# A new order of work, five residual buffers and one output tile in two halves, in a retention-then-gMLP kernel on one core

## The chip, the cores and the metric

The kernel runs on one core of one Trainium2 chip. The metric is the device time of one execution in microseconds (us); a smaller time is better. The time of the kernel before is the median of 11 runs.

## The reference

Two layers, one after the other. The first is a retention layer: for 8 batches and 8 heads, with sequences of 576 rows and head dimension 64, scores of q and k are weighted with a decaying causal mask and multiplied with v. Its result, with the heads put side by side, is x, of 576 rows by 512 columns for each batch. The second is a gMLP block on x.

```python
scores = scale * np.matmul(q, k.transpose(0, 1, 3, 2))
Dmat = np.where(rel >= 0, gamma[:, None, None] ** rel[None, :, :], 0.0)
attn = np.matmul(scores * Dmat[None], v)
x = attn.transpose(0, 2, 1, 3).reshape(B, S, H * D)
h = gelu_tanh(x @ w_in)                      # 512 -> 1024
u, vv = h[..., :512], h[..., 512:]
v_n = layer_norm(vv) * g_ln
v_s = np.einsum('ts,bsd->btd', w_sg, v_n) + b_sg[None, :, None]
out = x + (u * v_s) @ w_out                  # 512 -> 512
```

All inputs and the output are float32; the kernel computes the products in bfloat16 and adds up in float32.

## The kernel before, in words

**Tiling.** The 8 batches are taken in 4 pairs p = 0 to 3. A pair has 1152 rows, that is 9 row tiles of 128, so there are 36 row tiles i = 0 to 35 in all (tile i belongs to pair i // 9). The retention layer works in 5 blocks for each pair, b = 0 to 19 in all. Four blocks of a pair cover 256 rows of one batch; the third one (b = 2, 7, 12, 17) covers the last 64 rows of one batch and the first 64 of the other.

**The steps.** The texts below name them so:
- load: the rows of q, k or v of one block go from DRAM to a tile `ld` (lines 431 and 434; 12 buffers). prep: GpSimd (POOL) scales and casts them to bfloat16 (lines 457 and 463; VectorE and ScalarE do q and k of block 0).
- T(b), copied by Tev: TensorE transposes q and k (line 503), VectorE copies the result from PSUM to `qkT` (line 512). From block 15 on (TB = 15), a DMA transpose TX(b) on SP's queue does both (line 519).
- S(b,g): scores (line 543); VectorE multiplies them with the mask, Sev (lines 556 and 559). Z(b): the running state of keys times values (line 577), with its sums on VectorE. O(b) and O2(b): the output of the block (line 626). Oev: ScalarE copies it to `xT` (line 682), which holds the x of a whole pair, transposed, in 2 buffers.
- V(i) and U(i): the two halves of x @ w_in (lines 693 and 740); ScalarE applies gelu (lines 700 and 750). VectorE takes the statistics (708), POOL turns them into scale and bias (713 to 716), ScalarE normalizes (728, and 725 for the tile in which the two batches of a pair meet).
- W(e,c,half): the product with w_sg (line 759); VectorE multiplies it with u, Wg (line 769).
- out(i): the product with w_out (line 786). For pair 0, x is added by TensorE (line 781). For tiles 9 to 35, X(i), a DMA transpose on SP's queue (line 795), brings the x of the tile back to row order, into `xr`, and VectorE adds it while it copies from PSUM, Oev of the output (line 802). `xr` has three buffers. store(i): SP's queue writes the finished tile of 128x512 float32 to DRAM (line 806).
- The five pieces of w_sg are loaded (lines 388 and 393), cast by ScalarE (line 397), transposed on TensorE (line 867, "builds of wT") and copied by VectorE (871). w_in comes in two halves: the half for V (in `wst`) and the half for U (in `uT`), each cast half by VectorE (371) and half by ScalarE (373).

**What sets the order.** Every step is a job with an engine, its dependencies and the buffers that it takes. A planner in the kernel's source (class `Planner`) can order them by a cost model. Here it doesn't: a string `ORDER` of 900 numbers is given, and each engine executes its jobs in the sequence in which their numbers stand in the string. Each engine, and SP's queue too, takes its instructions strictly in that sequence, so that a job that waits holds up all jobs behind it on its engine. Items like "f13" in the string are fillers: matmuls on a constant tile (line 338) that keep TensorE busy while nothing else can be done. PSUM gives the steps T, S and O two double-bank buffers ("pp") and all other TensorE steps four single-bank ones ("d").

Of the kernel before, what the change touches and what calls it, by code (L numbers as in the profile page):

```python
# [15 lines left out]
Alu = mybir.AluOpType  # L16
# [3 lines left out]
FETCH = ((32000.0, 7200.0), (130000.0, 6000.0), (1e9, 4800.0))  # L20
# [5 lines left out]
    '0 f9 1 2 81 8 111 83 6 f11 84 112 7 82 114 113 85 115 3 f2 87 13 86 116 122 118 117 278 f13 17 119 120 12 88 279 '  # L26
    'f3 280 121 281 9 123 282 23 124 f5 283 24 284 4 298 5 127 299 14 128 300 285 22 129 89 288 130 125 126 132 133 '
    '11 301 25 10 134 302 286 291 303 287 136 289 32 80 304 33 135 293 137 290 313 294 292 295 f2 15 90 f1 16 139 34 '
    '131 314 305 140 36 138 311 306 296 307 321 143 318 35 322 144 319 145 312 308 324 320 323 360 309 141 146 361 '
    '297 328 310 362 325 329 142 315 148 326 37 19 f4 149 18 21 363 327 20 38 152 364 330 366 91 99 92 95 365 97 100 '  # L30
    '26 93 316 98 373 147 43 96 317 94 370 153 374 367 331 154 27 39 150 380 151 42 371 375 155 368 381 332 376 156 '
    '334 333 369 342 40 382 335 343 157 372 383 338 384 158 377 340 385 28 41 430 339 341 161 29 159 163 431 389 44 '
    '379 160 336 390 386 378 162 164 46 107 387 392 47 337 31 388 347 432 391 30 433 393 348 45 166 396 108 434 167 '
    '351 435 172 436 49 349 397 344 165 350 352 398 50 354 345 173 101 174 355 170 102 168 353 171 450 48 440 179 451 '
    '437 441 504 169 452 443 438 180 439 453 444 51 175 442 58 454 105 456 394 106 455 447 176 470 182 53 177 188 449 '
    '465 178 471 472 395 457 183 466 356 189 463 458 346 448 508 459 460 190 464 357 461 181 473 358 186 474 359 187 '
    '109 476 445 475 52 54 110 103 446 477 56 104 462 184 478 191 185 467 516 399 59 517 414 400 197 518 416 192 468 '
    '409 57 469 407 415 410 198 60 519 417 195 536 520 537 206 401 521 408 405 196 522 523 402 427 479 524 406 482 '
    '193 428 200 194 429 480 62 199 201 403 481 529 404 525 526 207 530 418 527 528 538 419 483 202 420 591 203 539 '
    '63 215 421 55 540 592 61 533 411 422 541 542 217 593 534 424 216 66 412 545 543 535 544 209 67 546 204 210 425 '  # L40
    '484 550 208 68 205 548 551 547 594 549 71 485 213 552 631 595 214 488 596 492 632 423 489 597 500 633 64 493 553 '
    '611 501 211 222 218 212 413 598 531 612 599 231 76 554 600 502 496 613 490 503 532 486 219 223 491 601 426 487 '
    '65 224 614 602 225 603 615 604 617 226 78 608 616 75 621 605 606 232 609 622 220 227 221 607 618 70 228 494 619 '
    '634 495 677 73 620 229 240 635 626 678 505 230 627 233 637 509 679 506 636 561 623 497 242 510 573 511 498 69 '
    '562 680 507 241 234 575 697 628 681 698 624 683 512 574 682 559 243 258 610 565 560 625 690 248 566 629 235 557 '
    '630 638 249 684 639 691 640 236 685 238 499 692 558 643 567 239 687 251 237 641 688 555 686 642 693 699 556 246 '
    '752 247 700 576 701 702 753 513 644 77 689 568 577 694 709 569 579 514 254 710 244 570 256 695 703 245 72 250 '
    '706 704 255 578 696 571 587 707 711 705 754 515 645 572 583 712 708 563 74 661 713 79 647 662 564 755 646 257 '
    '715 648 252 772 253 259 756 588 757 773 580 758 714 759 581 262 589 584 657 760 774 765 665 585 263 651 766 582 '
    '762 264 590 652 761 265 726 763 663 727 764 732 649 769 775 650 664 260 792 733 776 724 777 794 270 658 793 725 '  # L50
    '744 770 666 659 778 586 271 779 771 667 261 273 655 780 716 656 734 717 795 735 268 781 838 796 745 797 839 798 '
    '799 269 787 668 800 746 660 782 801 748 653 783 747 804 767 788 673 784 785 654 669 789 805 266 274 749 275 840 '
    '272 768 674 267 786 670 790 675 791 802 750 671 740 276 803 858 277 841 736 720 859 722 676 728 860 723 721 842 '
    '751 861 843 718 672 844 845 719 862 853 848 854 846 806 849 847 741 863 729 850 737 807 855 742 864 730 818 738 '
    '814 856 731 822 743 865 808 834 857 823 815 812 809 826 810 867 811 739 813 824 866 868 816 825 819 817 869 870 '
    '820 874 827 871 821 835 830 828 876 872 836 875 837 851 873 829 883 889 852 879 897 881 880 884 877 882 831 878 '
    '890 832 833 898 891 901 887 899 892 895 888 900 893 896 909 885 894 905 886 902 910 903 904 906 911 907 912 908 '
# [8 lines left out]
class Job:  # L66
    def __init__(self, eng, dur, due, fn, deps=(), new=None, uses=(), mode=None, nbytes=0, run=0, what="", behind=None, since=0.0, lag=0.0, ins=0, port=False, parts=1):
        self.what, self.behind, self.since, self.lag, self.ins, self.port, self.parts = what, behind, since, lag, ins, port, parts
        self.eng, self.dur, self.due, self.fn = eng, dur, due, fn
        self.deps = [d for d in deps if d is not None]  # L70
        self.new = [] if new is None else list(new) if isinstance(new, (list, tuple)) else [new]
        self.mode, self.nbytes, self.run = mode, nbytes, run
        self.start = self.out = None
        for b in uses:
            b.users.append(self)
        for b in self.new:
            b.users.append(self)


class Planner:  # L80


    def __init__(self, bufs, free, slack=60.0, penalty=500.0, fill=None, fill_until=0.0):
        self.bufs, self.free = bufs, free
        self.slack, self.penalty = slack, penalty
        self.fill, self.fill_until = fill, fill_until
        self.jobs, self.order = [], {t: [] for t in bufs}
        self.dma_free, self.dmas, self.ring = 0.0, [], []
        self.mode, self.warm = None, False
        self.count, self.block, self.landed = 36, 1, 0.0  # L90
        self.port = 0.0

# [38 lines left out]
    def place(self, j, t):  # L131
        j.start = t
        if j.nbytes:
            n = j.nbytes / j.run / 16.0 / j.parts
            at = t
            for part in range(j.parts):
# [8 lines left out]
                self.dma_free = max(self.dma_free, at + 1500.0) + (9.5 + 0.0385 * j.run) * n  # L145
# [3 lines left out]
                self.dmas.append(j.out)  # L149
            self.free[j.eng] = at  # L150
# [83 lines left out]
def kernel(  # L234
# [12 lines left out]
    nc = tc.nc  # L247
# [18 lines left out]
    BUFS = dict(ld=12, wst=1, qkb=2, vb=3, qkT=3, ret=4, zb=4, zs=3, xT=2, uT=2, vg=3, mv=3, vn=10, ob=3, xr=3,  # L266
# [506 lines left out]
    def m_O(i):  # L773
# [4 lines left out]
        r = slice(128 * m, 128 * m + 128)  # L778
        if p < XP:
            for j in range(KK):  # L780
                ins = nc.tensor.matmul(op[:, 128 * j:128 * j + 128], xTs[p][:, m, j, :], ident[:],
                                       start=(j == 0), stop=False, skip_group_check=True)
                if j == 0:
                    mark(ins, ("out", i))
# [12 lines left out]
    def m_Oev(i):  # L797
        op, ob = cur.pop(("op", i)), cur["ob", i]
        if i // NT < XP:
# [5 lines left out]
    def m_store(i):  # L805
        nc.sync.dma_start(outf[128 * i:128 * i + 128, :], cur.pop(("ob", i))[:])
# [119 lines left out]
    for b in range(NBL):  # L926
# [12 lines left out]
        if b < TB:  # L939
            tpb = Buf("pp")  # L940
            jT = add("PE", 565.0 * h, t0, lambda b=b: a_T(b), deps=[jq, jk], new=[tpb, B_qkT[b]], uses=[B_qkb[b]], mode="Q", ins=33 * ns)
            jTe = add("DVE", 90 + 1130.0 * h, t0 + 700.0, lambda b=b: a_Tev(b), deps=[jT], uses=[tpb, B_qkT[b]])
        else:
            jTe = add("SP", 2400.0 * ns, t0, lambda b=b: a_TX(b), deps=[jq, jk], new=[B_qkT[b]], uses=[B_qkb[b]],
                      nbytes=262144 * ns, run=256)
# [9 lines left out]
    for b in range(NBL):  # L955
# [13 lines left out]
        if n == 2:  # L969
            jc = add("ACT", 380.0, jz.due + 300.0, lambda b=b: a_Zcv(b), deps=[jz], new=B_zb[b], uses=zd)  # L970
            ja = add("DVE", 330.0, jz.due + 300.0, lambda b=b: a_Zadd(b), deps=[jz], new=B_zs[b], uses=zd)
            J["zb", b, 1] = jc
        else:
            ja = add("DVE", 660.0 if len(cs) == 2 else 330.0, jz.due + 300.0, lambda b=b: a_Zadd(b), deps=[jz] + prev,
                     new=[B_zb[b]] + ([B_zs[b]] if n != 4 else []), uses=zd + ([B_zs[b - 1]] if prev else []))
            J["zb", b, 0] = J["zb", b, 1] = ja
            if n != NBK - 1:
                jc = add("ACT", 380.0 if n == 1 else 597.0, jz.due + 900.0, lambda b=b: a_Zcv(b), deps=[ja], uses=[B_zb[b], B_zs[b]])
# [58 lines left out]
        if n in (2, NBK - 1):  # L1037
# [12 lines left out]
            for u in order:  # L1050
# [13 lines left out]
                else:  # L1064
# [11 lines left out]
                    else:  # L1076
                        xr = Buf("xr")
                        jX = add("SP", 1000.0, due - 6000.0, lambda i=i: m_X(i), deps=J["xd", i], new=xr, uses=[B_x],
                                 nbytes=131072, run=256)
                        jOut = add("PE", 862.0, due, lambda i=i: m_O(i), deps=need + wo, new=[db, obb],  # L1080
                                   uses=[B_u], mode="F", ins=9)
                        jOe = add("DVE", 640.0, due + 700.0, lambda i=i: m_Oev(i), deps=[jOut, jX], uses=[db, obb, xr])
# [32 lines left out]
```

## Time and profile before

| | |
|---|---|
| median of 11 runs | 213.28 us (211.26 to 216.53) |
| the profiled execution, its own time | 212.12 us |
| its span in the profile | 210.4 us |
| TensorE (PE) busy | 197.1 us, 94% |
| VectorE (DVE) busy | 152.8 us, 73% |
| ScalarE (ACT) busy | 119.4 us, 57% |
| GpSimd (POOL) busy | 113.3 us, 54% |
| DMA, mean | 231 GB/s, 48.64 MB |

The profile is of one execution. The span runs from the first to the last instruction of that execution; its own time is 1.72 us longer. "PE" is TensorE's matmuls, "SPq" SP's DMA queue. A group of instructions is named by source line, engine, operation and tiles. In a list of waits, "A <- B: 11.1, 3, 4.0" says that A waited for B 11.1 us in total, in 3 places, 4.0 us in the longest. In a timeline, the first number is the start, the second the duration, and what stands in brackets is how long the engine sat idle before it and what ended that.

### The profile page before, as it was taken

What the parts mean: (1) busy time and instruction counts of PE and PEld (TensorE: products, weight loads), DVE (VectorE), ACT (ScalarE), POOL (GpSimd) and SP (SyncE); (2) the same over time, 40 slices, a digit from 0 to 9 for tenths busy, and PEclk for the clock granted to TensorE, in tenths of its full rate; (3) what the DMA queues carried; (4) which work ended last, traced back from release to release, by engine and by line L of the source; (5) the groups of instructions that cost most, each with busy time, mean ns of one, the idle gap of its engine ahead of it and who ended that gap; (6) DMA issues with size and microseconds to landing.
All of it is one profiled execution on the core that took longest, in us unless ns stands there. A gap on an engine that the chain in (4) does not pass through costs nothing.

```text
span 210.4 us, 7861 instructions
## 1 busy us (share of the span) xinstructions
PE 197.1 (94%) x3378; PEld 131.1 (62%) x3378; DVE 152.8 (73%) x293; ACT 119.4 (57%) x198; POOL 113.3 (54%) x157
## 2 busy tenths in 40 slices
PE   7998669999999999999999999999799999999982
PEld 3555356577666767675876676758375657566750
DVE  5876558779858769873995885998667886568463
ACT  3215898894885775459665528485526384533300
POOL 5390369796579788557579498256096080012000
PEclk9999999999999999999999999999999999999999
DMA  5999999999999999999999989999788937254565
GB/s 163 290 333 226 321 239 337 299 309 254 201 260 288 262 270 263 235 263 293 274 258 265 306 216 233 196 202 223 178 229 184 219 103 126 101 153 144 158 199 174
DMA packets 94117, 48.64 MB, mean 231 GB/s; under 512 B 38202, under 2 KB 87362, under 8 KB 94082
## 3 DMA queue, kind: packets, MB, share of 16 engines
q1 hardware_dynamic: 94064, 48.13, 94.0%
q8 instruction: 26, 0.43, 1.0%
q14 instruction: 9, 0.07, 0.1%
q10 hardware_dynamic: 18, 0.00, 0.0%
HBM read 32.79 MB, written 9.44 MB: 201 GB/s over the span
## 4 chain that ended last, share of the span: by engine, by line
PE 67%; DMA 9%; SPq 7%; DVE 7%; POOL 4%; ACT 3%; issue 2%; DVEq 0%; ACTq 0%; POOLq 0%
PE wp L759 17%; PE op L786 12%; PE hv L693 11%; PE hu L740 11%; PE pp L626 6%; DMA uT<-in_moe_w_in_dram 5%; SPq L431 4%; PE pp L543 3%; PE pp L503 3%; DMA qkT<-qkb 2%; DMA xr<-xT 2%; DVE bst L708 2%; PE zd L577 2%; DVE ret L556 2%; PE wtp L867 1%
## 5 line engine op out<-in xcount | busy, mean ns | idle before, releaser
L463 POOL TENSOR_TENSOR qkb<-ld,gqv 128x1024 bf16<-128x1024 f32 (+1 forms) x19 | 32.7, 1723 | 21.9 <-DMA ld<-in_q_dram 9.7
L556 DVE TENSOR_TENSOR ret<-pp,msk 128x1024 bf16<-128x1024 f32 x32 | 38.6, 1219 | 5.6 <-PE pp L543 5.4
L759 PE MATMUL wp<-wT,vn 128*128 128x288 bf16 x256 | 40.3, 286 | 0.0
L463 POOL TENSOR_TENSOR vb<-ld,gqv 128x1024 bf16<-128x1024 f32 (+1 forms) x20 | 34.5, 1732 | 8.1 <-DMA ld<-in_v_dram 8.1
L740 PE MATMUL hu<-xT,w_in 128*128 128x256 bf16 (+1 forms) x320 | 37.0, 262 | 1.9 <-ACT xT L682 1.9
L682 ACT ACTIVATE xT<-pp 128x512 bf16<-128x512 f32 (+1 forms) x40 | 24.8, 672 | 23.8 <-PE pp L626 21.7
L693 PE MATMUL hv<-w_in,xT 128*128 128x512 bf16 x144 | 36.2, 380 | 1.8 <-ACT xT L682 1.1
L786 PE MATMUL op<-w_out,uT 128*128 128x512 bf16 x144 | 34.9, 379 | 0.7 <-DVE uT L769 0.6
L769 DVE TENSOR_TENSOR uT<-wp,uT 128x288 bf16<-128x288 f32 x64 | 27.2, 448 | 11.4 <-PE wp L759 11.2
L708 DVE BATCH_NORM_STATS2 bst<-vg 128x6 f32<-128x512 f32 x36 | 24.7, 685 | 12.2 <-ACT vg L700 12.1
L740 PEld LDWEIGHTS <-w_in 128*128 128x128 bf16 x320 | 28.0, 98 | 8.7 <-issue 2.1
L700 ACT ACTIVATE vg<-hv 128x512 f32<-128x512 f32 x36 | 21.2, 596 | 16.4 <-PE hv L693 11.5
L759 PEld LDWEIGHTS <-vn 128*128 128x128 bf16 x256 | 24.8, 98 | 8.1
L728 ACT ACTIVATE vn<-vg,mv 128x512 bf16<-128x512 f32 x32 | 25.3, 808 | 6.8 <-POOL mv L716 6.7
L713 POOL TENSOR_SCALAR mv<-mv 128x2 f32<-128x2 f32 (+1 forms) x20 | 4.5, 225 | 42.8 <-DVE mv L709 42.3
L750 ACT ACTIVATE uT<-hu 128x512 bf16<-128x512 f32 x36 | 20.9, 594 | 11.3 <-PE hu L740 11.0
L693 PEld LDWEIGHTS <-xT 128*128 128x128 bf16 x144 | 13.2, 98 | 14.5 <-ACT xT L682 2.1
L786 PEld LDWEIGHTS <-uT 128*128 128x128 bf16 x144 | 13.3, 98 | 13.8 <-DVE uT L769 1.0
L802 DVE TENSOR_TENSOR ob<-op,xr 128x512 f32<-128x512 f32 x27 | 17.9, 687 | 5.5 <-PE op L786 5.4
L512 DVE COPY qkT<-pp 128x2048 bf16<-128x2048 bf16 (+1 forms) x15 | 16.6, 1108 | 4.7 <-PE pp L503 4.7
L457 POOL CAST qkb<-ld 128x1024 bf16<-128x1024 f32 (+1 forms) x19 | 18.0, 947 | 1.7 <-DMA ld<-in_k_dram 1.7
L759 PE MATMUL wp<-wT,vmid 128*128 128x288 bf16 x64 | 17.9, 287 | 0.0
(89 smaller groups left out, 235.1 us busy)
## 6 DMA issues: line engine op xcount, KB each, us to landing
out_dram<-ob SPq DMA_DIRECT2D x36, 256.0 KB, 4.2
ld<-in_q_dram SPq DMA_DIRECT2D x16, 512.0 KB, 7.1
ld<-in_k_dram SPq DMA_DIRECT2D x16, 512.0 KB, 6.1
ld<-in_v_dram SPq DMA_DIRECT2D x16, 512.0 KB, 7.1
wst<-in_moe_w_sg_dram SPq DMA_DIRECT2D x2, 576.0 KB
wst<-in_moe_w_in_dram SPq DMA_DIRECT2D x1, 1024.0 KB
ld<-in_k_dram SPq DMA_DIRECT2D x8, 128.0 KB, 4.8
ld<-in_q_dram SPq DMA_DIRECT2D x8, 128.0 KB, 7.2
```

Of the source, the lines that this page charges most:

```text
L463: eng.tensor_tensor(dst, src, g.unsqueeze(3).to_broadcast(list(src.shape)), op=Alu.mult)
L556: ins = nc.vector.tensor_tensor(ret[:].rearrange("p r (k t) -> p (r k) t", k=2), sc[:].rearrange("p r (k t) -> p (r k) t", k=2), msk2[:].r ...
L682: nc.scalar.activation(dst, src, Act.Copy)
L693: ins = nc.tensor.matmul(hv[:], xTs[p][:, m, kk, :], w_in[:, kk, F2:], start=(kk == 0), stop=(kk == KK - 1))
L700: unfence(nc.scalar.activation(vgs[i][:], cur.pop(("hv", i))[:], Act.Gelu_apprx_tanh), ("V", i))
L708: nc.vector.bn_stats(bst[:], vgs[i][:])
L728: nc.scalar.activation(vn[:], vg[:], Act.Identity, scale=mv[:, s, 2:3], bias=mv[:, s, 3:4])
L740: ins = nc.tensor.matmul(hu[:, n, :], w_in[:, kk, 128 * c:128 * c + 128], xTs[p][:, m:m + w, kk, :], start=(kk == 0), stop=(kk == KK - 1), ...
L750: unfence(nc.scalar.activation(uTs[p][:, c0:c1, 128 * m:128 * m + 128 * w], cur.pop(("hu", i, half))[:], Act.Gelu_apprx_tanh), ("U", i, half))
L759: ins = nc.tensor.matmul(ps[:], vns[t0 + j][e][:, 128 * c:128 * c + 128], wT[e][j][:, half * HS:(half + 1) * HS], start=(j == 0), stop=(j ...
L769: ins = nc.vector.tensor_tensor(uTs[p][:, c, col:col + HS], cur.pop(("wp", b, c, half))[:], uTs[p][:, c, col:col + HS], op=Alu.mult)
L786: ins = nc.tensor.matmul(op[:], uTs[p][:, c, r], w_out[:, c, :], start=(p >= XP and c == 0), stop=(c == KK - 1), skip_group_check=True)
```

## The change

1. `xr` has five buffers in place of three.
2. Tile 34 (`NP * NT - 2`) gets its output in two halves of 256 columns: eight matmuls of 256 columns in place of four of 512, two additions on VectorE in place of one, and two stores, one from ScalarE's queue and one from SP's.
3. `ORDER` is another string. Nearly all lines of it differ; the set of jobs is the same. The fillers are 9, 11, 5, 17, 4, 5 and 3 in place of 9, 11, 2, 13, 3, 5, 2, 1 and 4 units.
4. The planner's cost model has other numbers (among them a term for the switch between copies and transposes in the DMA queue). As `ORDER` is given, the model only sets the sequence in which the source writes the jobs of different engines down, not the sequence on an engine.

The diff, with the order string left out:

```diff
-FETCH = ((32000.0, 7200.0), (130000.0, 6000.0), (1e9, 4800.0))
+FETCH = ((32000.0, 7000.0), (130000.0, 5500.0), (1e9, 4700.0))
+XBAR = 500.0
...
 ORDER = (
...
-                self.dma_free = max(self.dma_free, at + 1500.0) + (9.5 + 0.0385 * j.run) * n
+                self.dma_free = max(self.dma_free, at + 1500.0) + (XBAR if j.xb and not self.xb else 0.0) + (9.5 + 0.0395 * j.run) * (1.0 if j.parts == 1 else 1.35) * n
...
-    BUFS = dict(ld=12, wst=1, qkb=2, vb=3, qkT=3, ret=4, zb=4, zs=3, xT=2, uT=2, vg=3, mv=3, vn=10, ob=3, xr=3,
+    BUFS = dict(ld=12, wst=1, qkb=2, vb=3, qkT=3, ret=4, zb=4, zs=3, xT=2, uT=2, vg=3, mv=3, vn=10, ob=3, xr=5,
...
     def m_O(i):
...
+        if i == NP * NT - 2:
+            for hf in range(2):
+                for c in range(KK):
+                    ins = nc.tensor.matmul(op[:, 256 * hf:256 * hf + 256], uTs[p][:, c, r], w_out[:, c, 256 * hf:256 * hf + 256],
+                                           start=(c == 0), stop=(c == KK - 1), skip_group_check=True)
+            return
...
     def m_Oev(i):
         op, ob = cur.pop(("op", i)), cur["ob", i]
+        if i == NP * NT - 2:
+            xr = cur.pop(("xr", i))[:].rearrange("p j r -> p (j r)")
+            for hf in range(2):
+                r = slice(256 * hf, 256 * hf + 256)
+                nc.vector.tensor_tensor(ob[:, r], op[:, r], xr[:, r], op=Alu.add)
+            return
...
     def m_store(i):
-        nc.sync.dma_start(outf[128 * i:128 * i + 128, :], cur.pop(("ob", i))[:])
+        ob = cur.pop(("ob", i))
+        if i == NP * NT - 2:
+            for hf in range(2):
+                r = slice(256 * hf, 256 * hf + 256)
+                (nc.scalar, nc.sync)[hf].dma_start(outf[128 * i:128 * i + 128, r], ob[:, r])
+            return
+        nc.sync.dma_start(outf[128 * i:128 * i + 128, :], ob[:])
...
-            jTe = add("SP", 2400.0 * ns, t0, lambda b=b: a_TX(b), deps=[jq, jk], new=[B_qkT[b]], uses=[B_qkb[b]],
-                      nbytes=262144 * ns, run=256)
+            jTe = add("SP", 1350.0 * ns, t0, lambda b=b: a_TX(b), deps=[jq, jk], behind=J["T", b - 1] if b == TB else None, new=[B_qkT[b]], uses=[B_qkb[b]],
+                      nbytes=262144 * ns, run=256, xb=True)
...
-                        jX = add("SP", 1000.0, due - 6000.0, lambda i=i: m_X(i), deps=J["xd", i], new=xr, uses=[B_x],
-                                 nbytes=131072, run=256)
+                        jX = add("SP", 1200.0, due - 6000.0, lambda i=i: m_X(i), deps=J["xd", i], new=xr, uses=[B_x],
+                                 nbytes=131072, run=256, xb=True)
```

The orders of the two built programs differ, among others, here (the sequence on each engine, by job):

```
SP, before: ... X14 X12 TX15 store9 X13 TX16 load19q X15 store13 load17k store14 X17 store12 X16 load18q load19v TX17 ...
SP, after:  ... X11 X9 X12 X10 load16q load15v X13 store9 load16v load17k load16k TX15 store11 store10 store12 X14 X17 X15 TX16 X16 load17q ...
SP, after:  ... load19q X20 X18 TX18 store15 store19 TX19 load19v X25 ...
ACT, before: prepk0 Zcv0 Oev0 Oev0 w_in(V) Zcv1 w_sg(4) vmid w_in(U) gelu0 Oev1 gelu1 Oev1 ...
ACT, after:  prepk0 Zcv0 vmid w_in(V) Oev0 Oev0 Zcv1 gelu0 gelu1 Oev1 w_in(U) Oev1 ...
PE, before, last: ... W(7,3,1) W(7,2,1) W(7,0,1) out33 out35 out34
PE, after, last:  ... W(7,2,1) W(7,3,1) W(7,0,1) out33 out34 out35
```

TensorE changes 76 times between the steps T, S, Z, O and the others, in either order.

## The prediction

> **What bounds the kernel now.** I read the page's busy table and slices first, then the chain of work that ended last, then the timeline where the chain leaves TensorE, then the waits.
>
> ```profile
> PE 197.1 (94%) x3378; PEld 131.1 (62%) x3378; DVE 152.8 (73%) x293; ACT 119.4 (57%) x198; POOL 113.3 (54%) x157
> ...
> PE   7998669999999999999999999999799999999982
> ...
> GB/s 163 290 333 226 321 239 337 299 309 254 201 260 288 262 270 263 235 263 293 274 258 265 306 216 233 196 202 223 178 229 184 219 103 126 101 153 144 158 199 174
> ```
>
> Each digit is a slice of 5.26 us. TensorE has gaps in slices 1 to 6 (0 to 32 us), one dip at 147 us, and a tail. In the start its digits flatter it: the fillers (line 338) are 14.6 us of its 197.1. So the start is fed by DMA, and from 41 us on TensorE is the bound.
>
> ```profile
> 15.22 9.50 DMA uT<-in_moe_w_in_dram
> 24.75 1.06 ACT w_in L373
> 25.82 1.28 ACT L700
> 27.11 0.61 ACT vg L700
> ...
> 145.10 4.11 DMA xr<-xT
> 149.36 0.75 ACT xT L682
> 150.15 1.04 PE hv L693 x4
> ```
>
> The chain shows two places to win. In the first, ScalarE waits for the U half of w_in with the gelus behind it. In the second, a copy-transpose X that lands at 149.2 holds ScalarE's Oev, and with it TensorE. The waits put a price on the second and name its cause:
>
> ```profile
> PE hv L693 <- ACT xT L682: 1.1, 1, 1.1
> ...
> SPq L795 <- DVE ob L802: 11.1, 3, 4.0
> ```
>
> Line 795 issues X: three times SP stood still until VectorE freed an xr buffer, 11.1 us in all.
>
> How full is TensorE afterwards? From the chain I take the pace of each step back to back (W 0.61, V, U and out 0.87, O 0.57, T 0.57, S 0.24, Z 0.25 us, a block of 128 rows about half). The jobs from U(5) on, at 43.2 us, add up to 153.9 us in either order, and 56 changes of step at some 0.13 us to 7.3. TensorE ends at 206.4, after 163.2 us. So only 163.2 - 153.9 - 7.3 = 2.0 us of stalls are left there. **No order can win more than about 2 us after 43 us**; the rest must come from the start.
>
> **What the Trainium skill says.** "PSUM — Partial Sum Buffer", section "Engine vs sequencer instructions": the queues of ScalarE, VectorE and GpSimd are strictly first in, first out. The trace agrees: hv of tile 0 was done at 20.6 us, yet its gelu ran at 27.11, behind the cast that waited for DMA until 24.75. "DMA: Bandwidth & Descriptors", section "Issuing engines are not separate DMA queues": a DMA issued from another engine runs on the same 16 DMA engines and saves only the time on the sequencer. Here an issue of a store takes SP 0.53 us (median of line 806), so half a store on ScalarE's queue is worth at most that. "Perfetto Trace Analysis", section "Tensor Engine Instruction (MATMUL, LD_WEIGHTS)": TensorE's ends are estimated; hence I count pace, not busy time.
>
> **The start.** On ScalarE the new order puts gelu 0, gelu 1 and the first Oev of block 1 ahead of the cast of w_in(U). They had waited behind it. V(0) now waits for Oev of block 0, which stands behind the cast of w_in(V): that ends at 19.9, Oev at 20.6, V(0) at 21.7, and with the table load (1.28 us) gelu 0 can run at about 23 in place of 27.1. POOL gets q and k of block 1 before its v, so T(1) needn't wait for one prep (1.9 us); q, v and k of block 2 come together. This frees some 3 us on those engines. It is not all kept. What next binds is w_sg: the builds of wT need all its casts, and those need its DMA. The loads ahead of it are the same set in both orders: 9744 KB = 9.98 MB up to its end. The first seven slices of the GB/s row sum to 1909 GB/s, times 5.26 us 10.04 MB at 36.8 us, so its last byte moves at about 36.7. From bytes to landing I take k of block 3: 6.96 MB, moved by 26.2 (five slices, 7.01 MB), landing at 28.92 (POOL waits for it): 2.6 us. So w_sg lands at 39.3.
>
> ```profile
> 28.92 1.04 POOL L457 CAST qkb<-ld 128x1024 bf16<-128x1024 f32 x1 [0.32 <-DMA ld<-in_k_dram]
> ...
> 38.79 2.39 ACT L397 ACTIVATE wnat<-wst 128x576 bf16<-128x576 f32 x4
> ...
> 41.66 1.57 PE L867 MATMUL wtp<-ident,wnat 128*128 128x128 bf16 x25
> ```
>
> The two last casts (0.6 us each, 2.39 / 4) end at 40.5, and with 0.2 to hand over the builds start at 40.7 in place of 41.66: **0.9 us**. TensorE is ready for them by then: k of block 4 (8.80 MB, moved by 33.2) lands at 35.8, is cast by 36.9, and T(4), O(3), O2 and S after it take 1.5 us. With the shorter lag that the U half of w_in shows (5.91 MB by 22.9, landing 24.75: 1.85 us) w_sg lands at 38.5 and the gain is 1.7. If the casts queue behind gelus, it is 0.3. I take 0.9 and keep 0.3 to 1.7. Fillers rise from 50 to 54 units; they are placed before O2(1), where TensorE waits for w_in anyway, so I cost them at nothing. If that cover fails, 4 units are 4 x 14.6 / 50 = 1.2 us.
>
> **Five xr buffers.** Their gain is in the order behind them. Before, SP's queue held X14, X12, X13, X15, X17 and X16 each until the output three X earlier had been added, and X16 came last, after out(13). The transposed x of pair 3 takes the xT buffer of pair 1, whose last reader is X16. So X16, issued at 145.10 behind X15, X17, three stores and a load, held the Oev of block 15, which TensorE had finished at 147.2; V(27) started at 150.15, where TensorE had idled 1.1 us. After, X16 needs only the buffer of X10, whose out(10) stands some 22 us of TensorE work ahead of O(15). The wait goes, **1.1 us**. What is late next there is ScalarE: V(27) follows O2(15) by 1.5 us of work and Oev takes 0.75 and two hand-overs, so nothing is left over, and nothing is missing. In a stretch where TensorE is the bound the gain lasts to the end, unless SP's queue takes it back (below). Bounds: 0 to 1.1.
>
> SP moves more than this. X11, X9, X12 and X10 now stand in one run ahead of loads of blocks 15 and 16, at 1.22 us of issue each, about 5 us. POOL's preps of those blocks come late in the order too (TensorE needs them some 15 us on), so I cost it at nothing; without that cover it is up to 5 us.
>
> **The halves.** They are cut into tile 34, which was the last one before. In the new order tile 35 is the last, whole, on TensorE, VectorE and SP. So here **the change doesn't do what it says**: the end stays an addition of 0.69 us at 206.65 and a store until 210.4. The price of the halves: eight matmuls of 256 columns go at the pace of four of 512 (U: 0.87 for eight, V: 0.86 for four); two additions of 256 columns at 0.42 (line 604 has that size) in place of 0.69, so 0.15 us more on VectorE, while out(35) takes 0.86 on TensorE; ScalarE has had no work since 196.4. Zero; at worst 0.15. Had it hit the last tile, it would have saved 0.69 - 0.42 = 0.27.
>
> **The sum.** 0.9 + 1.1 = 2.0 us off the profiled execution's own time: 212.12 - 2.0 = 210.1. That execution is 1.16 us below the median shown, so I take the same 2.0 from the median: 213.28 - 2.0 = **211.3 us**.
>
> **Rivals.**
> 1. *Nothing stays.* The DMA delivers no byte sooner (its busy share is 1.14 from 36.8 to 44 us), so TensorE, 0.9 us early, waits for v of block 4 or for block 5; and the stalls that the new order makes elsewhere take the place of the 1.1. For it: only 2.0 us of stall were left, and a new order has some of its own. Against: after 45 us POOL waited for DMA rarely. 213.28 - 2.0 + 0.9 + 1.1 = 213.3.
> 2. *SP holds up block 19: slower.* Before, v of block 19 was loaded at 148, and TX19 was ahead of store19. Now store19 stands before TX19, and load 19v behind it. From the end of out(19): addition 0.9, store 0.53, TX19 1.9 of issue, the load up to 7 us to landing, prep 1.9: 12.2 us. TensorE has 13.7 us of work and five changes of step (0.65) until Z(19) needs it. It decides once VectorE or SP is more than 2.1 us late there. SP's longest wait for VectorE was 4.0 us; if TX19's issue also takes its longest, 3.65, the delay is 4.0 + 1.75, and the stall 3.7 us. With the same lateness at blocks 17 and 18 costing a little: 211.3 + 4.0 = 215.3.
> 3. *The start gives more*, 1.7, the 1.1, and the rest of the 2.0 us (0.9) with some 0.8 at the tail's wait for Wg: 213.28 - 4.5 = 208.8. Against: the last W group stands as before.
>
> **Numbers.** Forecast 0.42 (its own range 210.2 to 212.2), rival 1 0.25, rival 2 0.21, rival 3 0.12. A difference of about 0.5% (1.07 us) is what a measurement here can tell from no change. Faster: 0.42 + 0.12 = 0.54, less 0.01 for the forecast's upper edge, 0.53; same 0.26; slower 0.21. The range leaves out half of rival 2 and half of rival 3: 209.0 to 215.2.
>
> **What would show it.** Gelu 0 near 23 us and the builds of wT near 40.7; no idle TensorE at V(27); SP's waits at line 795 for VectorE's additions well under 11.1 us; the last addition whole, some 2 us before 206.65. I am wrong if the builds start at 41.7 or later, if TensorE idles more than 2 us in total after 45 us, or if Z(19) or S(19) waits for POOL or for TX19.

## The result and the profile after

The changed kernel takes 210.21 us (median of 12 runs, 208.86 to 214.47). In the same session the kernel before took 212.53 us (median of 47 runs; the 11 runs of the table above had 213.28). The ratio is 0.9887, with a 95% interval of 0.986 to 0.9914: 2.4 us of 212.53 are gone, where the prediction had 2.0. (A ratio here leaves out executions over 1.5% above the fastest of their kernel, so it isn't quite that of the medians.) A second measurement of the changed kernel, in another session, gave 0.9927 (0.9895 to 0.9959), which is 1.6 us. Differences under some 0.4% between two of these ratios are therefore not told apart here.

First the busy row and the slices of the page of the changed kernel. One slice is 5.2 us:

```profile
span 207.9 us, 7879 instructions
...
PE 197.1 (95%) x3382; PEld 132.1 (64%) x3382; DVE 153.1 (74%) x294; ACT 119.5 (57%) x198; POOL 113.7 (55%) x157
...
PE   7999998699999999999999999999999999899982
```

TensorE's busy time hasn't changed. The span is 2.5 us shorter. The low digits in slices 4 to 6 have become 9s, slices 7 and 8 have dips instead, and the dip at 147 us has moved to 177 us.

The start, in the chain of waits of the changed kernel:

```profile
31.88 7.28 DMA wst<-in_moe_w_sg_dram
39.21 0.56 issue
39.77 0.68 ACT wnat L401
40.50 1.46 PE wtp L889 x23
41.95 0.87 PE hu L744 x8
```

and ScalarE's timeline there (start, duration, in brackets the idle time before it and what ended it):

```profile
22.64 1.08 ACT L704 ACTIVATE vg<-hv 128x512 f32<-128x512 f32 x2
...
37.58 1.26 ACT L401 ACTIVATE wnat<-wst 128x576 bf16<-128x576 f32 x2 [0.55 <-DMA wst<-in_moe_w_sg_dram]
39.18 1.26 ACT L401 ACTIVATE wnat<-wst 128x576 bf16<-128x576 f32 x2 [0.35 <-DMA wst<-in_moe_w_sg_dram]
```

Gelu 0 runs at 22.64 instead of 27.11. What holds the chain is no longer the U half of w_in but w_sg, which lands at about 39.2. ScalarE waits for it twice, and 23 of the 25 matmuls of the builds of wT follow at 40.50 (the first two ran at 39.69). Before, the four casts ran without a gap from 38.79 and the builds followed at 41.66: there ScalarE was late; here the DMA is.

The second place. In the changed kernel's list of SP's waits no X waits for VectorE's output addition any more (before: 11.1 us at three places). What stands there is stores that wait for their own tile, and one TX:

```profile
SPq L828 <- DVE ob L818: 8.4, 8, 3.4
SPq L828 <- ACT ob L816: 6.8, 3, 4.9
...
SPq L523 <- POOL vb L467: 4.5, 1, 4.5
```

Busy time by stretch (stretch, its length, then busy us and number of instructions of PE, PEld, DVE, ACT and POOL, the granted clock, the DMA share and GB/s), first before, then after:

```profile
140.00:160.00 20.00, 18.93 (x282) 12.38 (x271) 14.98 (x30) 10.76 (x19) 12.57 (x17) 1.00 0.87 205
160.00:180.00 20.00, 19.74 (x346) 13.23 (x345) 15.15 (x27) 11.04 (x19) 5.97 (x11) 1.00 0.69 142
```

```profile
140.00:160.00 20.00, 20.00 (x314) 14.13 (x312) 14.14 (x27) 10.87 (x19) 13.79 (x17) 1.00 1.19 244
160.00:180.00 20.00, 18.37 (x329) 11.83 (x328) 14.65 (x27) 9.63 (x17) 5.56 (x11) 1.00 0.93 173
```

The 1.07 us of idle TensorE at V(27) are gone, and 1.63 us have appeared in the stretch behind it, where before had 0.26. TensorE's timeline shows two of its waits there, one for the transpose TX18 and one for a gelu:

```profile
162.33 0.42 PE L547 MATMUL pp<-qkT 64*64 64x128 bf16 x16 [0.34 <-DMA qkT<-qkb]
...
177.59 1.03 PE L744 MATMUL hu<-xT,w_in 128*128 128x256 bf16 x8 [1.06 <-ACT vg L704]
```

The chain of the changed kernel tells where the second comes from:

```profile
164.11 0.46 issue
...
164.80 6.38 DMA xr<-xT
...
171.31 0.69 DVE ob L818
...
174.09 0.58 POOL mv L718
...
175.31 0.80 issue
176.11 0.81 ACT vmid L729
176.94 0.61 ACT vg L704
177.59 1.03 PE hu L744 x8
```

X25 stands in SP's queue behind TX19 and the load of v of block 19, and takes 6.4 us to land (the median of X in the list of DMA issues of before is 2.4). VectorE waits 1.30 us for it with the addition of tile 25, and the statistics of tile 31 stand behind that addition. So POOL, the two normalizations of the middle tile (1.63 us) and gelu 32 are late in turn, and U(32) finds TensorE idle for 1.06 us.

The end is as before: the last addition is whole, at 204.23 us. From the last run of out matmuls to the end of the span it is 207.9 - 201.42 = 6.48 us, before 210.4 - 203.85 = 6.55.

### The profile page after: what moved, and what is told of

Read it like the earlier page. It is cut to its first block, busy times and chain, and to the rows that moved or that the text cites. A ratio compares the mean times of both kernels' runs of the same rounds, so it can differ in the third digit from the quotient of the medians.

```text
span 207.9 us, 7879 instructions
## 1 busy us (share of the span) xinstructions
PE 197.1 (95%) x3382; PEld 132.1 (64%) x3382; DVE 153.1 (74%) x294; ACT 119.5 (57%) x198; POOL 113.7 (55%) x157
## 4 chain that ended last, share of the span: by engine, by line
PE 68%; DMA 12%; SPq 8%; DVE 3%; POOL 3%; issue 2%; ACT 2%; DVEq 0%; POOLq 0%; ACTq 0%
PE wp L763 16%; PE hu L744 13%; PE hv L697 12%; PE op L796 11%; PE pp L630 5%; SPq L438 4%; SPq L435 4%; DMA wst<-in_moe_w_sg_dram 4%; PE pp L547 3%; DMA xr<-xT 3%; DMA qkT<-qkb 3%; PE pp L507 3%; DMA ld<-in_k_dram 2%; PE zd L581 1%; PE wtp L889 1%
## 5 line engine op out<-in xcount | busy, mean ns | idle before, releaser
L712 DVE BATCH_NORM_STATS2 bst<-vg 128x6 f32<-128x512 f32 x36 | 24.7, 686 | 8.8 <-ACT vg L704 8.2
```

The lines of the kernel that those rows point to most:

```text
L712: nc.vector.bn_stats(bst[:], vgs[i][:])
```

## Experiments

All ratios are against the kernel before, run on the same chip in the same session.

**Five buffers alone** (b_xr5), in the old order:

```diff
-ob=3, xr=3,
+ob=3, xr=5,
```

> The kernel before with five xr buffers and nothing else changed (its order, its whole tiles). Theory: X16 no longer stands behind an X that waits for VectorE's addition, so SP's waits at line 795 for line 802 fall from 11.1 us to under 4, TensorE doesn't idle 1.1 us at V(27), and the time falls by about 1.1 us, ratio near 0.995. Rival: the buffers are worth nothing by themselves (the gain is one of order alone, or TensorE waits next for something else): ratio within 0.9985 to 1.0015.

Measured: 0.9955 (0.9929 to 0.9981), 0.95 us. The row that had 18.93 us of busy TensorE before now reads

```profile
140.00:160.00 20.00, 20.00 (x285) 13.00 (x274) 15.78 (x31) 11.25 (x20) 13.45 (x16) 1.00 0.99 233
```

and SP no longer waits for an addition at line 795. Nothing but the number of buffers differs, so the stall at V(27), 1.07 us, was X16's wait for a buffer. This is shown. What the profile also shows is a new wait in front of it: the first S on the product of TX16 (S of block 16), which before began at 139.56 without a wait.

```profile
139.49 0.64 PE L543 MATMUL pp<-qkT 64*64 64x128 bf16 x32 [0.53 <-DMA qkT<-qkb]
```

**The new start alone** (b_start): the new order up to U(5), the old one from there, three buffers.

> The new order up to the end of the builds of wT(0) (all jobs before U(5)), then the remaining jobs in the order of the kernel before; three xr buffers, whole tiles. Theory: the start gives about 1.3 us, which TensorE, the bound afterwards, keeps to the end: ratio near 0.994, U(5) at 41.9 us in place of 43.2. Rival (nothing stays): DMA feeds blocks 4 and 5 no sooner and the gain is given back by 60 us: ratio 0.998 to 1.002.

Measured: 0.9966 (0.9939 to 0.9993), 0.7 us; half of what was expected. The builds ran at 40.61 and 41.07. SP still waited 10.0 us for additions, but of the 1.31 us of idle TensorE at 140 to 160 us only 0.41 stand at V(27); 0.90 stand at the same S of block 16, and a longer stall stands at a Z:

```profile
53.06 0.25 PE L577 MATMUL zd<-vb,qkb 64*64 64x64 bf16 x6 [1.36 <-issue]
...
141.18 0.64 PE L543 MATMUL pp<-qkT 64*64 64x128 bf16 x32 [0.90 <-DMA qkT<-qkb]
...
151.11 1.04 PE L693 MATMUL hv<-w_in,xT 128*128 128x512 bf16 x4 [0.41 <-ACT xT L682]
```

The profile names no cause for the stall at the Z. It comes after 26 of the 32 matmuls of this Z. The kernel before stops 0.45 us in the same Z, after 27, and b_start5 below, whose order is the same up to there, doesn't stop at all. So it belongs to this execution, and the start isn't shown to have made it.

**The old start with the rest new** (a_oldstart): the old order up to U(5), the new one from there, five buffers, halves.

> The counterpart: the order of the kernel before up to U(5), then the new one; five xr buffers and the halves as in the kernel after. Theory: it loses the start's 1.3 us and keeps the rest, about 1.1 us off the kernel before: ratio near 0.995. Rival (all comes from the start): ratio near 1.0. Rival (the start gave nothing): ratio 0.989, as the kernel after.

Measured: 0.995 (0.992 to 0.998), 1.1 us. Five buffers alone give as much. So, with the old start, the new order after U(5) adds nothing to the buffers that these runs can tell.

**Both terms of the sum without the new order behind U(5)** (b_start5): as the new start alone, with five buffers.

> The new order up to the builds of wT(0), the remaining jobs in the order of the kernel before, five xr buffers, whole tiles: the two parts that the prediction counted and nothing of the new order after 43 us. Theory: the parts add up as measured alone, 0.7 + 0.95 us, ratio near 0.992. Rival (the new order after 43 us gives more of its own): the difference between this and the kernel after (0.989) is what that order gives, more than 0.6 us. Rival (the parts hide each other): ratio 0.9955 as with either alone.

Measured: 0.9976 (0.9943 to 1.0009), half a microsecond. By the sum of the two parts it should have had 0.992, which the interval leaves out. But 0.992 carries the noise of both parts, and these were measured on another chip: the shortfall of 0.0055 is hardly more than the 0.005 that the three intervals leave together. The ratio alone doesn't prove that the parts fail to add up. TensorE's timeline shows where a gain is lost in the old order:

```profile
63.52 0.45 PE L577 MATMUL zd<-vb,qkb 64*64 64x64 bf16 x32 [1.10 <-POOL vb L463]
...
139.85 0.64 PE L543 MATMUL pp<-qkT 64*64 64x128 bf16 x32 [1.01 <-DMA qkT<-qkb]
```

The Z runs at 62.84 without a wait when only the buffers are changed; here POOL's v is 0.7 us later. The buffers have no part in this, as the first X goes out only at 67.48. In b_start, the same order up to there, POOL's work in front of that v waited 1.14 us for its load of q; so DMA is the likely cause, but POOL's v differs by as much between profiles of the old start (it ends at 63.7 in the kernel before).

The S is the one of block 16 again. It needs TX16, which SP issued at 134.22 in the kernel before and at 134.26 here, though TensorE was 1 us ahead of before in an S shortly ahead of it (129.76 in place of 130.77). So what TensorE had won by then, here and in b_xr5, it waits off at this place. (In b_start it was behind by then, and TX16 went out at 135.78.) The new order issues TX16 at 132.62, and its S, at 140.61, doesn't wait.

**The halves** (a_whole, a_last): tile 34 whole again; or the halves moved to the true last tile.

```diff
-        if i == NP * NT - 2:
+        if i == -1:
```

> The kernel after with tile 34 in one piece. Theory: the halves are cut into a tile that is not the last, so they are worth nothing: ratio as the kernel after, 0.989, within 0.15 us, and the last addition at the same time after the last matmul. Rival (the halves shorten the tail): 0.3 us slower than the kernel after.

```diff
-        if i == NP * NT - 2:
+        if i == NP * NT - 1:
```

> The kernel after with the halves cut into tile 35, which is the last one in the new order, in place of tile 34. Theory: the end gets shorter by one addition of 256 columns (0.69 - 0.38 = 0.3 us) at most, ratio to before near 0.9875 against 0.989 of the kernel after. Rival: the store's time from issue to landing sets the end and doesn't shrink, or the two halves' additions each wait for all eight matmuls: no difference from the kernel after.

Measured: 0.9853 (0.98 to 0.9907) and 0.9888 (0.9847 to 0.9929): both as the changed kernel. The tail, counted as above, is 6.57 us with no halves, 6.48 on tile 34, 6.40 on tile 35. The profile of the run with halves on tile 35 is of the longest of its six executions (span 211.1 us), so only its tail is read:

```profile
206.44 1.04 PE L786 MATMUL op<-w_out,uT 128*128 128x256 bf16 x8
...
207.51 0.76 DVE L813 TENSOR_TENSOR ob<-op,xr 128x256 f32<-128x256 f32 x2 [0.18 <-PE op L786]
207.97 0.38 ACTq L826 DMA_DIRECT2D out_dram<-ob  x1
208.29 0.33 SPq L826 DMA_DIRECT2D out_dram<-ob  x1
```

VectorE's first half does not start when TensorE's first half is done. It starts when all eight matmuls are done (at 207.48). In the changed kernel tile 34 shows the same: its eight matmuls end at 203.33, its first addition starts at 203.37. So only the first store leaves earlier, and what is left is under 0.2 us, less than the runs can tell.

**Four buffers** (a_xr4), the changed kernel otherwise. (No run has three: in the new order X10 would then wait for an output that needs loads behind X10 in SP's queue, so by the listing it could not go on.)

```diff
-ob=3, xr=5,
+ob=3, xr=4,
```

> The kernel after with four xr buffers (with three its order comes to a dead end, as X10 would wait for an output that needs loads behind X10). Theory: X13 waits for the addition of tile 11 and the loads of block 16 stand behind it on SP's queue for some 10 us, so blocks 15 and 16 come late and TensorE idles: 1 to 4 us slower than the kernel after. Rival: there is room enough in front of block 15 (15 us of TensorE work), no difference from the kernel after, and four buffers were enough.

Measured: 1.0003 (0.9973 to 1.0032): all of the gain is lost. SP's waits and TensorE's timeline of this kernel:

```profile
SPq L805 <- DVE ob L818: 7.3, 4, 2.7
...
SPq L523 <- POOL mv L720: 6.2, 1, 6.2
SPq L805 <- DVE zs L608: 5.4, 1, 5.4
```

```profile
147.79 0.44 PE L581 MATMUL zd<-vb,qkb 64*64 64x64 bf16 x32 [1.62 <-POOL vb L467]
166.10 0.42 PE L547 MATMUL pp<-qkT 64*64 64x128 bf16 x16 [0.87 <-DMA qkT<-qkb]
180.91 1.03 PE L744 MATMUL hu<-xT,w_in 128*128 128x256 bf16 x8 [0.79 <-ACT vg L704]
```

With one buffer too few, X waits for additions again, and the loads and TX behind it on SP are late: TensorE stalls at a Z that lacks its v, at an S that lacks its transpose, and at a U, 3.3 us in all. The S and the U wait in the changed kernel too, for 0.34 and 1.06 us, so 1.9 us of it are new. In the old order two buffers more were worth 0.95 us; in the new order one buffer is worth about 2.

**The stall that the change made** (a_stats31): VectorE takes the statistics of tile 31 ahead of the addition of tile 25.

```diff
-DVE: ... addition25 Wg Wg stats31 ...
+DVE: ... stats31 addition25 Wg Wg ...
```

> The kernel after with one job moved on VectorE: the statistics of tile 31 go ahead of the addition of tile 25. In the kernel after that addition waits 1.30 us for X25, which waits in the DMA queue behind TX19, and statistics, POOL's scale, the normalization of tile 31 on ScalarE, gelu 32 and TensorE's U(32) (idle 1.1 us at 177.6) wait behind it. Theory: this chain is what takes back a part of the gain after 160 us; without it the time falls by about 1.1 us, ratio near 0.984. Rival: TensorE waits next for X25's own tile or for block 19, and the time stays within 0.3 us of the kernel after (0.989).

Measured: 0.986 (0.9818 to 0.9902). The stall at U(32) is gone; from 160 to 185 us TensorE waits only 0.30 us at 162.48 and 0.34 at 181.96. Each of the eight other profiles with this stretch of the new order has the stall at U(32), of 0.56 to 1.06 us. So the chain over X25 and stats 31 is shown. Its worth in time isn't: the point is 0.6 us below the changed kernel's, inside the interval. With tile 34 whole as well (**a_best2**) it was run once more, beside the changed kernel unchanged (**a_again**):

> The kernel after with tile 34 whole and the statistics of tile 31 ahead of the addition of tile 25 on VectorE. Theory: as a_stats31, some 0.6 us under the kernel after run beside it, ratio near 0.986. Rival: the same as the kernel after.

> The kernel after, unchanged, once more beside the others: both theories expect a ratio within the interval of its first measurement, 0.986 to 0.991.

Measured: 0.9869 (0.9844 to 0.9895) and 0.9927 (0.9895 to 0.9959). By these ratios it is ahead on that chip, but its median over all executions, 210.85 us, isn't below the 210.67 of a_again, and it is no better than the changed kernel was in its first measurement. In its profile the stall at U(32) is gone as well; an S waits 1.10 us for TX18 in its place. No version here beats the changed kernel by more than the runs can tell.

**ScalarE's order at the start** (a_cast): one job is moved, the cast of the U half of w_in, ahead of gelu 0 and 1 as in the kernel before; all else is the changed kernel.

```diff
-ACT: ... Zcv1 gelu0 gelu1 Oev1 w_in(U) Oev1 ...
+ACT: ... Zcv1 w_in(U) gelu0 gelu1 Oev1 Oev1 ...
```

> The kernel after with one job moved on ScalarE: the cast of w_in(U) goes back ahead of gelu 0 and gelu 1. Gelu 0 then runs after 26.7 in place of 22.6 us. Theory: what binds the start is the landing of w_sg at about 39.2 us, so this costs less than 0.6 us. Rival: the early gelus are what made the start shorter, so the whole 1.3 us are lost, ratio near 0.995.

Measured: 1.02 (1.0146 to 1.0254), 216.35 us: by the ratios some 6.6 us over the changed kernel, and some 4.3 us slower than before. The expectation, under 0.6 us, failed by ten times. The timelines of ScalarE, VectorE and TensorE in this kernel (the profile is of the longest of its six executions, 218.42 us):

```profile
26.38 1.06 ACT L377 ACTIVATE w_in<-uT 128x1024 bf16<-128x1024 f32 x1 [5.08 <-DMA uT<-in_moe_w_in_dram]
...
28.75 1.09 ACT L704 ACTIVATE vg<-hv 128x512 f32<-128x512 f32 x2
```

```profile
29.38 0.69 DVE L712 BATCH_NORM_STATS2 bst<-vg 128x6 f32<-128x512 f32 x1 [6.28 <-ACT vg L704]
...
31.00 0.66 DVE L516 COPY qkT<-pp 128x1024 bf16<-128x1024 bf16 x1
```

```profile
31.72 0.43 PE L547 MATMUL pp<-qkT 64*64 64x64 bf16 x16 [4.61 <-DVE qkT L516]
```

and its stretches:

```profile
26.00:26.50 0.50, 0.50 (x5) 0.23 (x2) 0.00 (x0) 0.12 (x1) 0.00 (x0) 0.96 1.16 299
26.50:27.00 0.50, 0.50 (x2) 0.00 (x0) 0.00 (x0) 0.50 (x1) 0.00 (x0) 0.50 1.33 306
...
28.00:30.00 2.00, 0.00 (x0) 0.00 (x0) 0.62 (x1) 1.99 (x4) 0.00 (x0) 0.50 0.96 253
30.00:32.00 2.00, 0.28 (x16) 0.28 (x16) 1.93 (x7) 1.06 (x2) 0.74 (x2) 0.50 1.06 274
...
34.00:36.00 2.00, 2.00 (x11) 1.45 (x10) 0.17 (x1) 0.40 (x2) 2.00 (x2) 0.50 1.08 376
```

The new order issues the load of the U half later than the order before (here 18.79 in place of 15.22 us; it lands at 26.4 in place of 24.7). ScalarE waits 5.08 us for it, and behind the cast gelu 0 runs at 28.75. VectorE stands 6.28 us in front of its statistics, with the copy of block 2's q and k behind them, so TensorE stands still for 4.61 us, and POOL does no work for 6.72 us, until 31.18. And TensorE's granted clock, the third column from the end, falls to 0.50; it does so at about 26.5 us, before that stall, which begins at 27.1. U(5) starts at 49.93 us in place of 41.79, 8.1 us late. From there to the end the two kernels take the same: 216.7 - 49.93 = 166.8 us against 207.9 - 41.79 = 166.1. All of the loss is in the start.

**The same with VectorE's order mended** (a_cast2): the copy of block 2 also goes ahead of stats 0.

```diff
-DVE: ... stats0 stats1 Tev2 ...
+DVE: ... Tev2 stats0 stats1 ...
```

> As a_cast (the cast of w_in(U) ahead of gelu 0 and 1 on ScalarE), but on VectorE the copy Tev(2) goes ahead of the statistics of tiles 0 and 1, as in the kernel before. Theory: a_cast's loss of some 6 us was not the late gelus but VectorE's queue, where Tev(2) stood behind statistics that waited for them, so that TensorE idled 4.6 us for S(2) and then ran at a lower granted clock; with Tev(2) ahead, less than 1.5 us are lost against the kernel after, and the clock stays at 1.0. Rival: the late gelus by themselves cost the 6 us (through POOL's scale and the normalization).

Measured: 1.0129 (1.008 to 1.0178), 215.08 us. Some 1.5 of the 6.6 us came back, give or take 1.5; over 5 were expected to. The clock did not stay at 1.0 either. The copy now ran at 23.75, but TensorE stood still all the same, one step later:

```profile
30.11 1.89 PE L697 MATMUL hv<-w_in,xT 128*128 128x512 bf16 x4 [4.22 <-ACT xT L686]
```

This V needs Oev of block 1, and on ScalarE that stands behind the two gelus and the cast. So VectorE's copy was one of two jobs caught behind the wait, and mending it uncovered the other. The clock was at 0.50 from about 29.4 to 32.8 us, and U(5) came at 46.56; the rest took 213.1 - 46.56 = 166.5 us again.

## Why the prediction was right, and what stays open

**The start, 0.9 us.** The steps held: gelu 0 at 22.64 (said: near 23), w_sg landing at 39.2 (said: 39.3), the builds at 40.50 (said: 40.7). The size of the term is less sure than one profile suggests: with the old start the builds ran at 41.66 here, but at 40.90 in b_xr5 and 40.71 in a_oldstart. I take the start of U(5) in every profile but that of a_last, of kernels with the new ScalarE order and of kernels with the old start:

| U(5) starts at, us | |
|---|---|
| old start | 43.18, 42.41, 42.22; mean 42.6 |
| new start | 41.79, 41.45, 43.05, 41.62, 41.69, 42.44, 42.36, 41.92; mean 42.0 |

The same program differs by 1.3 us from one execution to another (41.79 and 43.05 are both the changed kernel; in the second, gelu 2 ran at 30.1 in place of 28.5). So the start is worth about 0.6 us in the mean, give or take some 0.4, within the bounds of 0.3 to 1.7. The two profiles shown, 43.18 and 41.79, flatter it. That it is worth something rests on the ratio of b_start, 0.7 us, whose interval ends at 0.9993.

**Fillers at nothing.** Four more units, and TensorE's idle time in the first 30 us still fell from 6.47 to 2.39 us. From 30 to 45 us it rose from 0.73 to 2.42, so TensorE had room behind the fillers too. Nothing speaks against the step; no run tests it alone.

**What is left after U(5).** The prediction said that no order could win more than about 2 us there. From U(5) to the end of the span the kernel before took 210.4 - 43.18 = 167.2 us, with five buffers alone 166.7, and the changed kernel 166.1, 165.7 (a_again) and 165.3 (tile 34 whole). That is 1.5 us in the mean: within the limit, and more than the 1.1 of the stall. But TensorE's idle time from 45 to 200 us fell only from 1.81 to between 1.35 and 1.77, and 0.45 of the 1.81 is the stop in a Z that has no cause in the profile. The other microsecond doesn't show as idle time in the records, and where it is stays open. The prediction named more than 2 us of idle TensorE after 45 us as a sign of being wrong. Counted up to TensorE's last matmul, the three profiles have 2.3, 1.9 and 1.5, the kernel before 2.4. So the first is over the mark: the stall at V(27) went, and others took its place.

**Five buffers, 1.1 us.** The mechanism was right, and alone it measured 0.95. What the prediction does not say is that the new order cannot do without them: with one fewer the whole gain is gone.

**The sum 0.9 + 1.1.** The 2.0 us lie between the two measurements of the whole, 2.4 and 1.6. With everything behind U(5) taken as one part, the parts measured alone add up to that as well: start 0.7, rest 1.1 (a_oldstart). The time itself, 210.21, is at the very edge of the forecast's own range, because the kernel before had a median of 212.53 over 47 runs and not 213.28. What the prediction did not have is that the sum depends on the order behind U(5). In the old order both parts together measured 0.5, and TensorE waited for TX16 at 140 us; the new order issues TX16 earlier. This share of the new order is read from the timelines, and no run moves TX16 alone. To that extent the sum came out by luck.

**The halves, nothing; cut into tile 34, which isn't the last.** Right. On the true last tile they would have brought 0.08 to 0.17 us of tail, less than the 0.27 written, because the first addition waits for all eight matmuls.

**The rivals.** *Nothing stays* is refuted for the changed kernel (the intervals end at 0.9914 and 0.9959). But what it describes happens: in the old order TensorE waits off its lead at block 16 (b_start5), and in the new one stalls of 1.06 and 0.34 us follow on the 1.07 that went. *SP holds up block 19* looked at the right queue and the wrong victim. Block 19's v came in time: POOL had to wait 1.00 us for it, and Z(19) waited for nothing. What came late behind TX19 was X25, and through VectorE's strict order it took 1.06 us at U(32), a price that the forecast had at zero. *The start gives more* had w_sg landing 0.7 us earlier than it did.

What the prediction did not see: that the place of one cast on ScalarE decides over some 6 us. It priced ScalarE's new order by what binds next, w_sg. That is right for the order as given. It says nothing of what happens if one job of that order is changed back, as the failed expectation of a_cast shows.

## What to carry to other kernels

In a hand-written order for engines that take their work strictly in sequence, one resource and one order belong together: price them together, and do not count on the parts adding up in another order, or on a single job being movable. Time that is won early is kept only if nothing behind it comes at a fixed time: look for the next transfer that TensorE will reach too soon. When a job is put in front of a wait, list everything behind it on that engine and on the engines that it feeds; the costs here came from the second and third engine, not from the first. And compare more than one profile before crediting a microsecond to a DMA-fed start, or charging a stall to an edit.

## What the hardware showed that was not expected

- TensorE's granted clock fell to 0.50 in two kernels with long stalls. In a_cast2 it was there from about 29.4 to 32.8 us, and fell 3.5 us into a stall of 4.22 us. In a_cast it was there from about 26.5 to 36.7 us, around a stall of 4.61 us, but it fell 0.6 us before that stall began, while fillers kept TensorE busy. So the stall didn't set it off; what did stays open. There 16 matmuls of U took 3.35 us in place of 1.91, so part of a_cast's price is this clock.
- The copy-transposes X landed 2.4 us after their issue at the median in the kernel before and 4.4 in the changed kernel, where they ranged from 2.4 to 7.6. A TX right ahead doesn't explain it by itself: the X issued right behind TX16 (134.00) took 4.4 us, and one behind a load (150.66) took 7.6.
- An addition on the first half of a PSUM tile, written by four matmuls, began only after the four matmuls of the second half, 0.03 us behind the last. Whether the chip or the waits in the program make it so, the runs don't settle.
